# Set-up of a Fourier mixing and gated feed-forward kernel: zeroed rows for halved tables, one product for channel 128, gathers ahead of weights

## The chip, the cores and the metric

The kernel runs on one core of a Trainium2 chip. A core has a matrix engine (TensorE, in the profile PE, with its weight loads as PEld), a vector engine (VectorE, DVE), a scalar engine (ScalarE, ACT), a general engine (GpSimd, POOL), a queue engine that only issues DMAs (SyncE, SP), and 16 DMA engines that all queues share. The metric is the time of one execution on the device in microseconds; lower is better. Each engine works through its own list in order, and semaphores tie the lists together.

## The reference

```python
# x: (8, 3008, 256) float32; w_gate, w_val: (256, 1536); w_out: (1536, 256)
X = np.fft.fft(x, axis=1)                 # along the sequence, 3008
X = np.fft.fft(X, axis=2)                 # along the channels, 256
x = X.real.astype(np.float32).reshape(8 * 3008, 256)
gate = np.maximum(x @ w_gate, 0.0)
val = x @ w_val
return (gate * val @ w_out).astype(np.float32)
```

## The kernel before, in words

**The algebra.** The real part of the two transforms is cosine times cosine minus sine times sine. Because cosine is even and sine odd, row s and row 3008 - s are first added or subtracted ("folded"), then the two halves of the sequence, then channel d and channel 256 - d. What is left is a product of folded rows (F for cosine, G for sine; bf16) with tables tabC and tabS. Its results are U and V, 128 channels by output frequencies. The transform along the channels is a small matrix (TA for cosine, TB for sine) that is multiplied into the weights once: WA = TA^T w and WB = TB^T w for gate and value. Then a tile of the feed-forward part is WA·U + WB·V, and the mirrored frequencies are WA·U - WB·V, made by adding a product with -2V (the tile VM, named CB in the profile) or with WM = -2WB on top of the first sum. Channel 128 has no partner; it is carried in row 0 of V, since row 0 of G is zero.

**Where things lie.** Rows of a half batch are spread over 128 partitions in three thirds t = 0, 1, 2, each with two rows a (or "par") in a partition: XD[p, r, t, a, d] holds row 1 + 2(128t + p) + a of half r, and XG holds the mirrored rows, with a reversed. AA is XG + XD. The last third has 120 partitions of rows and one more, 120, for row 0. Two rows are their own mirrors, row 752 (partition 119, a = 1) and row 0 (partition 120, a = 1). In the kernel before both XD and XG hold them, so they are counted twice, and ScalarE multiplies those two rows of the tables of column c = 5 (t = 2, par = 1) by a half: wv is 1 below partition 119 and 0.5 from there (lines 323 to 324 for the odd frequencies, 460 to 462 for the even ones, wv itself in lines 343 and 344).

**The set-up, in order of the lists.** The schedule is written out by hand; nothing reorders it. SP and ACT issue the upward rows and the plain rows of the first third, then SP the plain rows of the second third, row 0 twice (load_row_0), its mirror and a filling of the unused partitions 121 to 127. POOL makes index vectors and issues gathers of the mirrored rows (load_mirror, L117): two for the second third, then a memset of one element of XD (hold, L113), on which SP's load of the last third waits, then the first gate weights (load_w, L297), the two gathers of the last third, the first value weights, and later the rest of the weights and wo. The first third isn't gathered: TensorE turns it around by a product with a reversed unit matrix (turn, L351). VectorE computes quotients for the angles, md for TA and TB, and for each third AA (L405 or L415, and L406 or L416 for the two end channels), F for both halves (channels, L395 and L393) and G (channels_g, L399). TensorE makes the angles of the odd frequencies (angle, L315 and L316), ScalarE their sines and cosines (L319 to L321).

**The first transform** (dft_first, lines 556 to 614) makes U and V of batch 0 for the odd frequencies. It runs the thirds in order. In each third the list has products for U (k = 0, F with tabC), for V (k = 1, G with tabS) and the channel-128 products (nyquist, L570: one column of F as weights, output row 0 of V's bank), the latter for each half r. Because a channel-128 product may come first, V's banks are opened by two products with zeros (L592). combine (L586) makes the first third of WA and WB from the raw weights; both calls stand ahead of the last third's part. Then ScalarE copies one sum (es), VectorE adds and subtracts (L546) into U and V, and ScalarE makes VM for segment 0 from V (minus_v, L473). The first tiles (first_tile, L887 and L889) follow at once; the mirrored product of a tile (mirror, L804) needs VM.

**Behind it, on POOL.** Once VectorE is through with the thirds (it sets go, L420), POOL folds the even frequencies of batch 0 (lines 434 to 444) and then runs turns_and_rows: the rows of batch 1, the products kvec·us for the even tables (even_turns, L431 and L432), VM of segment 1 and the gathers of batch 1. The even tables are made between the first tiles, by VectorE (L456, L458) and ScalarE (L457, L459, and L461 for the halving). For later batches fold_steps issues load_rows and load_row_0 for the batch after.

Of the kernel before, what the change touches and what calls it, by code (L numbers as in the profile page):

```python
# [34 lines left out]
def kernel(  # L35
# [55 lines left out]
    def load_rows(b, ts=range(3)):  # L91
        for t in ts:
            n = (128, 128, 120)[t]
# [3 lines left out]
    def load_row_0(b):  # L97
        for r in range(2):
            nc.sync.dma_start(out=XD[120:121, r, 2], in_=dram(x, (b * S + r * H) * D, [[0, 1], [0, 2], [1, D]]))
# [4 lines left out]
    def load_spare():  # L104
        for X in (XD, XG):
            nc.sync.dma_start(out=X[121:128, :, 2, :, :].rearrange("p r a d -> p r (a d)"),
                              in_=dram(x, 512 * D, [[2 * D, 7], [H * D, 2], [1, 2 * D]]))
# [68 lines left out]
    def fold_steps(b):  # L176
# [15 lines left out]
        for t in range(3):  # L192
            for i in range(2):
                steps.append((1.1, lambda i=i, t=t: fold_pq(e, p, i, t)))
                if (t, i) == (1, 0) and b + 1 < B:
                    steps.append((0.0, lambda: (load_rows(b + 1), load_row_0(b + 1))))
# [22 lines left out]
    load_row_0(0)  # L219
# [14 lines left out]
    wv = single("wv", [128, 1])  # L234
# [59 lines left out]
    load_rows(0, (2,))  # L294
# [3 lines left out]
    load_w(0, 0)  # L298
    for r in range(2):
        load_mirror(0, 2, r)  # L300
    load_w(1, 0)
# [10 lines left out]
    def angle(n, c):  # L312
# [9 lines left out]
        if c == 5:  # L322
            for tab in (tabC, tabS):
                steps.append(lambda tab=tab: act(tab[r, 5, odd_k], tab[r, 5, odd_k], ACTF.Copy, scale=wv[r]))
# [12 lines left out]
    quotient(4)  # L337
    nc.vector.tensor_scalar(ums[:], pidx[:], scalar1=1.0 / D, op0=ALU.mult, scalar2=None)
# [4 lines left out]
    nc.vector.tensor_scalar(wv[:], pidx[:], scalar1=119.0, op0=ALU.is_lt, scalar2=0.5, op1=ALU.mult)  # L343
    nc.vector.tensor_scalar(wv[:], wv[:], scalar1=0.5, op0=ALU.add, scalar2=None)
# [51 lines left out]

    def channels_g(p, r, t):
# [3 lines left out]
    for t in range(3):  # L401
        n = ROWS[1][t]
        p = slice(0, n)
        if t:
# [3 lines left out]
            for r in range(2):  # L408
                channels(p, r, t)
            for r in range(2):  # L410
                channels_g(p, r, t)
        else:
            nc.vector.memset(GG[1][:].rearrange("p i t q d -> p (i t q) d")[:, :, 0:1], 0.0)
            for r in range(2):
# [3 lines left out]
                channels(p, r, t)  # L418
                channels_g(p, r, t)
# [14 lines left out]
    nc.gpsimd.tensor_copy(go[:, 1:2], go[:, 0:1])  # L434
    hold(slice(0, 3))
    nc.gpsimd.memset(GG[0][:].rearrange("p i t q d -> p (i t q) d")[:, :, 0:1], 0.0)
    for t in range(3):
        p = slice(0, ROWS[1][t])
        for i in range(2):
            nc.gpsimd.tensor_tensor(XG[p, i, t], AA[p, 0, t, :, D:0:-1], AA[p, 1, t, :, 0:D], op=SIGN[i])  # L440
# [676 lines left out]
```

## Time and profile before

| what | value |
|---|---|
| median of 3 runs | 636.41 us (636.18 to 636.57) |
| the profiled execution: its time, its span | 636.55 us, 634.8 us |
| instructions | 12470 |
| DMA | 66.38 MB, mean 105 GB/s |
| first product of the first DFT (L564) starts | 10.00 us |
| first product of the tiles (L887) starts | 19.99 us |
| first mirrored product, with VM (L804), starts | 21.87 us |
| wo asked for, landed | 15.46 us, 15.2 us later |

The span runs from the first to the last instruction in the record of one execution; the rest of that execution's time lies around it. Times of instructions below are counted from the start of the span. In a timeline a line gives start, length, engine, line of the kernel, operation, output and input, and in brackets how long the engine had been idle and what ended that; "issue" there means that nothing which the record shows ended it. Matmuls overlap, so their spacing, not their length, is what each costs.

### The profile page before, as it was taken

The numbers are of one execution on the slowest core, as the hardware profiler recorded it, in microseconds if no ns is written. First come the engines' busy times: TensorE is split into PE (matmuls) and PEld (weight loads), VectorE is DVE, ScalarE is ACT, GpSimd is POOL, SyncE is SP. The second block draws the span as 40 slices with busy tenths as digits, with TensorE's granted clock in tenths as the row PEclk, the third lists the DMA queues.
The fourth block names the chain that finished last, engine by engine and source line by source line (L and its number), as shares of the span: only waits on it lengthen the run. The fifth ranks groups of instructions, "written<-read, shape, count | busy, mean of one in ns | idle before, by whom it ended". The sixth has DMA issues, their size and how long they took to land.

```text
span 634.8 us, 12470 instructions
## 1 busy us (share of the span) xinstructions
PE 622.9 (98%) x4098; PEld 400.3 (63%) x4145; DVE 553.0 (87%) x981; ACT 449.1 (71%) x813; POOL 507.1 (80%) x494
## 2 busy tenths in 40 slices
PE   8999999999999999999999999999999999999997
PEld 3466666566666666666666666666666666666666
DVE  7896576998999999988999999898899989999991
ACT  7787667777777777777677777776777777777752
POOL 8986992898999998898889989699886566666660
PEclk9999999999999999999999999999999999999999
DMA  9953754615272426314272425311221111211122
GB/s 238 209 178 102 188 172 126 183 67 148 82 193 93 128 76 166 128 48 141 72 201 78 140 76 114 74 60 39 72 60 37 42 59 55 59 40 46 52 58 84
DMA packets 64017, 66.38 MB, mean 105 GB/s; under 512 B 19705, under 2 KB 46905, under 8 KB 63952
## 3 DMA queue, kind: packets, MB, share of 16 engines
q1 hardware_dynamic: 59536, 60.02, 33.1%
q0 software_dynamic: 3984, 4.92, 3.9%
q8 instruction: 32, 0.52, 0.4%
q10 hardware_dynamic: 432, 0.66, 0.3%
q14 instruction: 33, 0.27, 0.1%
HBM read 41.83 MB, written 34.13 MB: 120 GB/s over the span
## 4 chain that ended last, share of the span: by engine, by line
PE 91%; DVE 5%; issue 2%; ACT 1%; DVEq 0%; ACTq 0%
PE o L712 36%; PE v L799 10%; PE v L804 10%; PE g L938 8%; PE p L945 8%; PE v L798 7%; PE d L529 4%; DVE h L834 3%; PE p L804 1%; PE p L798 1%; PE p L799 1%; DVE r L949 1%; PE v L351 1%; DVE h L823 1%; PE d L640 0%
## 5 line engine op out<-in xcount | busy, mean ns | idle before, releaser
L950 POOL TENSOR_TENSOR r<-r 128x512 f32<-128x512 f32 (+1 forms) x252 | 314.3, 1252 | 99.8 <-DVE r L949 99.4
L834 DVE SCALAR_TENSOR_TENSOR h<-r,v 128x512 bf16<-128x512 f32 (+1 forms) x504 | 318.6, 674 | 40.0 <-PE v L804 27.9
L712 PE MATMUL o<-wo,h 128*128 128x256 bf16 x2172 | 330.9, 272 | 0.3 <-issue 0.3
L712 PEld LDWEIGHTS <-h 128*128 128x128 bf16 x2220 | 216.8, 98 | 113.7 <-issue 2.3
L933 ACT ACTIVATE p<-CB,b 128x512 f32<-128x512 bf16 (+1 forms) x252 | 172.5, 684 | 73.3 <-DVE r L949 71.7
L941 ACT COPY r<-g 128x512 f32<-128x512 f32 (+1 forms) x252 | 145.4, 577 | 66.9 <-PE g L938 58.7
L949 DVE SCALAR_TENSOR_TENSOR r<-r,p 128x512 f32<-128x512 f32 (+1 forms) x252 | 169.0, 670 | 0.6 <-ACT r L941 0.6
L799 PE MATMUL v<-V,WB 128*128 128x512 bf16 (+3 forms) x296 | 108.6, 367 | 2.3
L804 PE MATMUL v<-V,WM 128*128 128x512 bf16 (+1 forms) x252 | 94.4, 375 | 2.0 <-DVE h L834 1.6
L938 PE MATMUL g<-V,WM 128*128 128x512 bf16 (+1 forms) x252 | 94.5, 375 | 0.4 <-ACT r L941 0.3
L945 PE MATMUL p<-U,WA 128*128 128x512 bf16 (+1 forms) x252 | 94.5, 375 | 0.0
L798 PE MATMUL v<-U,WA 128*128 128x512 bf16 (+3 forms) x252 | 91.9, 365 | 0.0
L823 DVE TENSOR_TENSOR h<-r,v 128x376 bf16<-128x376 f32 (+1 forms) x88 | 45.1, 543 | 19.6 <-PE v L804 12.0
L798 PEld LDWEIGHTS <-WA 128*128 128x128 bf16 x347 | 33.8, 97 | 41.0 <-issue 12.3
L725 ACT COPY os<-o 128x512 f32<-128x512 f32 x92 | 52.5, 572 | 5.0 <-issue 4.5
L799 PEld LDWEIGHTS <-WB 128*128 128x128 bf16 x347 | 33.8, 97 | 34.1 <-DVE WB L385 0.6
L150 POOL TENSOR_TENSOR XG<-XG,XD 128x510 f32<-128x510 f32 x42 | 52.8, 1265 | 0.0
L814 ACT ACTIVATE r<-p 128x376 f32<-128x376 f32 (+1 forms) x80 | 38.2, 486 | 18.3 <-PE p L804 8.8
L158 POOL TENSOR_TENSOR AA<-XG 128x510 f32<-128x510 f32 x42 | 45.3, 1089 | 0.0
L938 PEld LDWEIGHTS <-WM 128*128 128x128 bf16 x252 | 24.6, 98 | 6.4 <-issue 1.0
L945 PEld LDWEIGHTS <-WA 128*128 128x128 bf16 x252 | 24.6, 98 | 3.4 <-issue 0.5
L804 PEld LDWEIGHTS <-WM 128*128 128x128 bf16 x252 | 24.6, 98 | 2.8
(182 smaller groups left out, 424.4 us busy)
## 6 DMA issues: line engine op xcount, KB each, us to landing
out_dram<-os SPq DMA_DIRECT2D x124, 128.0 KB
xr<-in_x_dram SPq DMA_DIRECT2D x12, 768.0 KB
XG<-xr SPq DMA_DIRECT2D x12, 768.0 KB
XD<-in_x_dram SPq DMA_DIRECT2D x15, 512.0 KB
out_dram<-os SPq DMA_DIRECT2D x35, 112.0 KB
XD<-in_x_dram SPq DMA_DIRECT2D x8, 480.0 KB
CB<-ch SPq DMA_DIRECT2D x7, 376.2 KB
out_dram<-os SPq DMA_DIRECT2D x13, 96.0 KB
```

What stands on the lines that cost most here:

```text
L150: e.tensor_tensor(XG[p, r, t, ::-1, 1:D], XG[p, r, t, ::-1, 1:D], XD[p, r, t, :, D - 1:0:-1], op=ALU.add)
L712: nc.tensor.matmul(st["p"][0:m, q, :], lhsT=lhs(f), rhs=wo[:, f, :], start=(f == 0 and not (early and q)), stop=(f == NF - 1), skip_group_ ...
L798: nc.tensor.matmul(bank[:, 0:st["n"]], lhsT=WA[i][:, st["f"]], rhs=st["us"], start=True, stop=False)
L799: nc.tensor.matmul(bank[:, 0:st["n"]], lhsT=WB[i][:, st["f"]], rhs=st["vs"], start=False, stop=True)
L804: nc.tensor.matmul(bank[:, 0:st["n"]], lhsT=W[i][:, st["f"]], rhs=v, start=False, stop=True, skip_group_check=True)
L834: nc.vector.scalar_tensor_tensor(half_h(st, sign), in0=st["s"][1 + sign][:, 0:n], scalar=0.0, in1=st["v"][:, 0:n], op0=ALU.max, op1=ALU.mult)
L933: nc.scalar.activation(st["p"][:, 0:st["n"]], st["c"], ACTF.Copy, scale=b2[:, st["fi"]:st["fi"] + 1])
L938: nc.tensor.matmul(st["g"][:, 0:n], lhsT=WM[0][:, st["f"]], rhs=st["vs"], start=True, stop=True)
L941: nc.scalar.copy(q[:, 0:n], st["g"][:, 0:n])
L945: nc.tensor.matmul(st["p"][:, 0:n], lhsT=WA[0][:, st["f"]], rhs=st["us"], start=False, stop=True, skip_group_check=True)
L949: nc.vector.scalar_tensor_tensor(sp[:, 0:n], in0=q[:, 0:n], scalar=-0.5, in1=st["p"][:, 0:n], op0=ALU.mult, op1=ALU.add)
L950: nc.gpsimd.tensor_tensor(sm[:, 0:n], sp[:, 0:n], q[:, 0:n], op=ALU.add)
```

## The change

- The halving of table rows goes: wv, its two instructions, and the four ScalarE operations that multiply tabC and tabS of c = 5. Instead XD is zero wherever XG already holds a self-mirrored row: VectorE zeroes XD[96:128, :, 2, 1, :] once, and the plain rows of the last third are loaded as 112 partitions of whole pairs (load_rows), then 8 partitions for a = 0 and 7 for a = 1 (load_last), so that partitions 119 and 120 of a = 1 stay zero in all batches. load_row_0 goes, load_last takes its place for every batch. For batch 0 the loads of the last third move behind the memset in the listing, in front of ums; the hold on POOL stays where it was.
- Channel 128 of both halves goes into one product: VectorE subtracts the two halves' channel 128 (half_128 into hy), ScalarE doubles the difference into bf16 (whole_128 into ny), and nyquist runs once for each third and par instead of once for each half too. The two products with zeros go; V's own first product opens its bank.
- The gathers of the last third are asked for ahead of the first gate weights on POOL.
- In dft_first the order is written anew: products loop over r outside and par inside; nyquist comes after U's products in the second and third thirds; combine(0) stays ahead of the last third, combine(1) goes into it in two parts; U is finished before V's last products are issued; WB of the gate is copied by VectorE, and WA of the value by ScalarE (before it was the other way around).
- VM of segment 0 is made by POOL, inside the fold of the even frequencies (fold_even, now called after dft_first), between its first and second operation, instead of by ScalarE.

```diff
     def load_rows(b, ts=range(3)):
-            n = (128, 128, 120)[t]
+            n = (128, 128, 112)[t]
...
-    def load_row_0(b):
-        for r in range(2):
-            nc.sync.dma_start(out=XD[120:121, r, 2], in_=dram(x, (b * S + r * H) * D, [[0, 1], [0, 2], [1, D]]))
+    def load_last(b):
+        for a in range(2):
+            n = (8, 7)[a]
+            nc.sync.dma_start(out=XD[112:112 + n, :, 2, a, :], in_=dram(x, (b * S + 1 + 2 * (256 + 112) + a) * D, [[2 * D, n], [H * D, 2], [1, D]]))
...
-                    steps.append((0.0, lambda: (load_rows(b + 1), load_row_0(b + 1))))
+                    steps.append((0.0, lambda: (load_rows(b + 1), load_last(b + 1))))
...
     hold(slice(2, 3))
-    load_rows(0, (2,))
...
-    load_w(0, 0)
     for r in range(2):
         load_mirror(0, 2, r)
+    load_w(0, 0)
     load_w(1, 0)
...
-        if c == 5:
-            for tab in (tabC, tabS):
-                steps.append(lambda tab=tab: act(tab[r, 5, odd_k], tab[r, 5, odd_k], ACTF.Copy, scale=wv[r]))
...
     quotient(5)
     quotient(4)
+    nc.vector.memset(XD[96:128, :, 2, 1, :], 0.0)
+    load_rows(0, (2,))
+    load_last(0)
...
-    nc.vector.tensor_scalar(wv[:], pidx[:], scalar1=119.0, op0=ALU.is_lt, scalar2=0.5, op1=ALU.mult)
-    nc.vector.tensor_scalar(wv[:], wv[:], scalar1=0.5, op0=ALU.add, scalar2=None)
...
+    def half_128(p, t):
+        nc.vector.tensor_tensor(hy[p, t], AA[p, 0, t, :, 128], AA[p, 1, t, :, 128], op=ALU.subtract)
+
+    def whole_128(t):
+        p = slice(0, ROWS[1][t])
+        nc.scalar.mul(ny[p, t], hy[p, t], 2.0)
...
             for r in range(2):
                 channels(p, r, t)
+            half_128(p, t)
...
+    def fold_even():
...
             for i in range(2):
+                if (t, i) == (0, 1):
+                    minus_v(nc.gpsimd, 0)
...
-        if c == 5:
-            steps += [lambda tab=tab: act(tab[r, 5, even_k], tab[r, 5, even_k], ACTF.Copy, scale=wv[r])
-                      for tab in (tabS, tabC)]
...
-        for par in (1, 0):
-            nc.tensor.matmul(bank[1, par][:, 0:NJ], lhsT=warm[:, 0:128], rhs=warm[:, 0:NJ], start=True, stop=False, skip_group_check=True)
-        part(0, (0,))
+        products(0, 0, (0,))
+        products(0, 1, (0,))
+        whole_128(0)
         angle(4, 5)
-        part(0, (1,))
+        products(0, 0, (1,))
+        products(0, 1, (1,))
+        nyquist(0)
         angle(5, 4)
-        part(1)
-        combine(0)
-        combine(1)
-        part(2)
+        whole_128(1)
+        products(1, 0, (0, 1))
+        nyquist(1)
+        products(1, 1, (0, 1))
+        combine(0, (0, 1))
+        whole_128(2)
         nc.scalar.copy(*whole(WA[0], raw[0]))
-        nc.vector.tensor_scalar(*whole(WA[1], raw[2]), scalar1=1.0, op0=ALU.mult, scalar2=None)
+        products(2, 0, (0, 1))
+        combine(1, (0,))
+        ends[0][1](1)
+        ends[0][1](0)
+        evict.pop(0)()
         nc.vector.tensor_scalar(m2[:], pidx[:], scalar1=1.0, op0=ALU.min, scalar2=-2.0, op1=ALU.mult)
...
+        sums[0]()
+        by_vector(WB[0], raw[1])
+        nc.scalar.copy(*whole(WA[1], raw[2]))
+        nyquist(2)
+        products(2, 1, (0, 1))
+        combine(1, (1,))
...
-        minus_v(nc.scalar, 0)
...
     dft_first(U, V)
+    fold_even()
     turns_and_rows()
```

## The prediction

> **What bounds the kernel now.** I read the engines' totals on the page first, then the chain that ended last, cut to the first 60 us because the whole diff lies there, then the timelines of VectorE and of GpSimd (POOL) in the set-up, and last the DMA queues microsecond by microsecond.
>
> ```profile
> PE 622.9 (98%) x4098; PEld 400.3 (63%) x4145; DVE 553.0 (87%) x981; ACT 449.1 (71%) x813; POOL 507.1 (80%) x494
> ```
>
> TensorE is busy for 98% of the span, so a microsecond by which its main stream starts earlier is a microsecond of the total, unless something else holds it later. The chain, from 16 us (start, length, what):
>
> ```profile
> 16.11 0.86 PE v L586 x4
> ...
> 17.24 0.59 PE d L586 x2
> 17.84 0.64 PE p L564 x4
> ...
> 20.26 0.56 DVE V L546
> 20.84 0.61 ACT CB L473
> 21.45 0.38 ACT r L814
> 21.87 0.32 PE p L804
> ...
> 43.70 0.48 ACT r L814
> 44.19 0.50 ACT tabS L461
> ...
> 46.86 0.32 PE p L804
> ```
>
> Two places are not TensorE alone: the hand-over from the first DFT to the tiles (VectorE makes V, ScalarE makes -2V into CB, then the first relu, then the mirrored product), and a ScalarE stretch at 43.7 to 46.9, in which TensorE sits idle for 0.28 and 0.39 us. Just ahead of 17.84 TensorE's weight load waits 0.2 us for VectorE's F of the last third: two chains arrive there almost together. VectorE's own side:
>
> ```profile
> 13.18 0.74 DVE L399 TENSOR_TENSOR G<-AA 128x254 bf16<-128x254 f32 x2
> 15.38 1.22 DVE L405 TENSOR_TENSOR AA<-XG,XD 121x1020 f32<-121x1020 f32 x1 [1.46 <-issue]
> 17.26 0.42 DVE L393 SCALAR_TENSOR_TENSOR F<-AA 121x258 bf16<-121x258 f32 x1
> ```
>
> It is done with the second third at 13.92 and waits 1.46 us, for nothing that an engine does: for data. POOL's timeline says which:
>
> ```profile
> 6.63 0.80 POOL L297 DMA_DIRECT2D h<-in_moe_w_gate_dram  x1
> 7.73 1.21 POOL L117 DMA_INDIRECT XG<-in_x_dram,gidx  x1 [0.30 <-issue]
> 9.24 0.98 POOL L117 DMA_INDIRECT XG<-in_x_dram,gidx  x1 [0.31 <-issue]
> 10.23 0.79 POOL L297 DMA_DIRECT2D h<-in_moe_w_val_dram  x1
> ```
>
> The last third's gathers are asked for behind the first gate weights, in one software queue. The two queues between 9 and 10 us (packets, MB, share):
>
> ```profile
> q1 hardware_dynamic: 112, 0.23, 97.9%
> q0 software_dynamic: 13, 0.01, 6.5%
> ```
>
> The last third's plain rows occupy 9 to 11.2 us; from 11.2 the software queue runs full, first in packets of about 1 KB (weights), from 12.5 to 14 in larger ones (gathers). VectorE starts 1.2 us after these end.
>
> **The change part by part.** All against the profiled execution: 636.55 us, span 634.8, so 1.75 around it; the median of the three runs is 636.41, 0.14 less.
>
> *Gathers first.* The weight issue in front of them took 0.80 us, so they are asked for at about 6.9 and 8.4 and the gate weights at 9.4; the second weight issue (10.23) and all behind it on POOL stay. What is surely gained is 0.8 us; with the weights' transfer (256 KB at the queue's 0.20 MB/us: 1.3 us) behind them too, the data could be there at 13.3. Landing is then 13.3 to 14.6; I take 14.0, the middle.
>
> *VectorE.* The added memset of 32x512 f32: the nearest row is 95x384 in 0.38, so 0.5 (bounds 0.21, the memset of 95x188, and 0.69, the longest 512-wide row nearby); the two wv operations removed give back 0.25. Both lie ahead of the 0.21 us for which L415 waits at 6.66 and the 0.65 us at 8.99, and are gone by then. It delays the absolute value for TA by 0.3 us on ScalarE, which has 0.83 us free at 8.8. Three half_128, 0.16 each by the 128x4 row of L416 (0.43 beside POOL work at most): two come before the last third, 13.92 + 0.3 = 14.2. So L405 starts at 14.25 instead of 15.38, and with the same spacing the last F stands at 16.55 instead of 17.68: 1.13 us.
>
> *SP.* The memset's wait queues load_rows of the last third and both load_last behind VectorE's 5.5; the hold on POOL releases at 6.68 as before (6.71 in the trace), so that wait costs nothing. The two load_last (16 and 14 rows of 1 KB, issue 0.56 to 0.79 by the row-0 loads that they replace) end by 8.3 and queue behind the plain rows, whose data end at 11.2; 3 us to spare before 14.25. For later batches it is five issues either way.
>
> *TensorE up to the last third.* Gone are two products with zeros (0.31 each, at half speed) and, in the first two thirds, four of eight channel-128 products (0.25 of spacing each); combine(1), 0.86, goes behind. Added: nyquist(1) waits for ScalarE's ny, a 0.2 us operation (row 128x1; 0.29 for 128x129) behind angle(5,4). Counting on from 9.38 at the trace's spacings: angle(4,5) done by 10.8, angle(5,4) by 12.3, then F of the second third (13.1, 13.45). ScalarE without the two halvings (0.52 and 0.50) ends the last table at 14.1, ny at 14.25; queued behind that wait are nyquist(1), products(1,1) and combine(0): 14.3 + 0.5 + 0.65 + 0.86 = 16.3. So TensorE is ready as F arrives (16.2 and 16.55).
>
> *The tail.* products(2,0) end at 16.95, combine (0.43) 17.4, two channel-128 products 17.8, products(2,1) 18.5, V's copy on ScalarE 18.9, V on VectorE 19.55 (the WB copy now ahead of it takes 0.65 that fits), the product that uses V at 19.6 instead of 20.86. ScalarE then has no -2V to make: the first relu runs at 20.0 to 20.45. POOL makes -2V in 0.57 (its row for segment 1), 19.6 to 20.2, in time. The mirrored product starts at 20.5 instead of 21.87: 1.37 us.
>
> *What POOL's wait delays.* POOL now stands from 18.9 to 19.6 for V with the rest of fold_even behind it: even_turns' first result comes at 31.65 instead of 31.29, and VectorE wants it (33.22 before) at 31.85. Cover: 0.2 us; without it every tenth goes to the products. wo lands at 30.66 and its first product would be at 31.1: 0.4 us of cover.
>
> *The weights' new place.* No row shows a weight transfer behind four gathers. Three weight rows land 6.0, 6.6 and 6.8 us after their issue: 15.4 to 16.2. TensorE wants them at 15.45, so the cost is 0 to 0.75; the queue holds the same bytes as it did when g4 landed at 15.38, so I take 15.6 and 0.15.
> On that the Trainium skill differs (DMA: Bandwidth & Descriptors, Anatomy of one DMA): about 2.0 us fixed plus bytes by 436 GB/s, an estimate of 2.6 us for 256 KB, which would land at 12.0 and cost nothing; the trace has 6.8 us for this transfer, and I keep to it.
>
> *Even tables.* Of the two removed ScalarE operations (L461) the first, 0.50, is in the chain. Behind it two copies of output (0.96) remain. Between 0 and the 0.67 us that TensorE idles there; I take 0.4.
>
> Sum: 1.37 - 0.15 + 0.4 = 1.6 us. 636.55 - 1.6 = 634.95 beside the profile, 634.8 beside the median. Bounds: 0.6 to 1.4 at the start and 0 to 0.67 at the tables, 0.6 to 2.1 together.
>
> **The rivals.**
>
> *The weights arrive last.* combine(0) now stands ahead of products(2,0), so a landing at 16.2 pushes everything by 0.75: 1.37 - 0.75 + 0.4 = 1.0, 635.4. For: 6.8 us is this very transfer's row, and 3.4 us passed between its issue and its first packets. Against: in those the plain rows had the engines.
>
> *POOL or the tables take it back.* VectorE waits 0.3 to 0.5 for even_turns, or the copies at 45.5 hold TensorE all the same: about 1.1 saved, 635.3. Against: POOL's wait is shorter than what VectorE's late start cost it before (1.12 at 18.44).
>
> *TensorE was the bound up to 17.8 and its savings are eaten by the wait for ny.* Only the tables remain: 636.0. Against: VectorE's 0.2 us at 17.7.
>
> *Slower: the clock drops.* The products of 376 columns start 0.31 us apart until about 10.0 and 0.16 from there, with granted clock 1.00 throughout; so there is a second, slower speed, and it lasted 8.8 us after the first product. The new order leaves TensorE idle at 12.3 to 13.1 and 13.75 to 14.3, where before it ran without a gap. If that sends it back to half speed for as long, 4.4 us are lost: 636.41 - 1.6 + 4.4 = 639.2. It decides (0.2%) from 2.9 us lost, that is 5.8 us at half speed. Against: 0.28 and 0.39 us idle at 45 to 47, and 0.46 at 4.1, were followed by no slower spacing than before.
> The Trainium skill (TensorE: Matmul & The Clock Gate, Part 1) has the rule: half clock after at least one idle window of about 3.4 us. By it gaps of 0.8 us change nothing; no gap so long is in this trace.
>
> **How the numbers follow.** 0.60 for the forecast, 0.15 for late weights, 0.06 for POOL or tables, 0.04 for TensorE as the bound, 0.15 for the clock and anything like it. About 0.2% (1.3 us) is what a measurement here can tell from no change; below 635.1 is faster, so faster 0.60, same 0.25, slower 0.15. The forecast's own range is 634.3 to 635.1, from the upper bound of the sum to the limit of what counts as faster. The whole range starts 0.3 lower, for the spread of the runs (636.18 to 636.57), and reaches to 637.7, where the slower case begins: 634.0 to 637.7 leaves that case's 0.15 out and a few hundredths below.
>
> **What would show it.** L405's second instance starting at 14.0 to 14.6 with under 0.5 us idle ahead of it; the first product with V near 19.6 and the mirrored one near 20.5; no TensorE idle of 0.3 us or more at 42 to 46. Against me: a wait of TensorE for weights at combine(0), VectorE waiting for AA from POOL near 32, or 0.31 us spacing after 12 us.

## The result and the profile after

The changed kernel takes 634.94 us (median of 10 runs, 634.55 to 635.49) where the kernel before takes 636.57 on the same chip (10 runs, 636.18 to 636.7). The ratio is 0.9975, with a 95% interval from 0.9965 to 0.9985. The profiled execution took 634.97 us with a span of 633.2, against 636.55 and 634.8 before: 1.6 us less in both, as forecast. The parts of that sum did not all come out as forecast, and some of them were not in it at all.

The totals of the engines, first part of the changed kernel's page:

```profile
PE 620.3 (98%) x4090; PEld 399.1 (63%) x4137; DVE 553.8 (87%) x983; ACT 446.8 (71%) x811; POOL 507.0 (80%) x495
```

TensorE has eight products fewer and is busy for 2.6 us less. Its share stays at 98%, so the span still follows the start of its main stream.

The chain that ended last, cut to 8 to 48 us (start, length, what):

```profile
8.19 4.82 DMA XG<-in_x_dram,gidx
13.00 0.67 DVE G L405 x2
13.67 0.37 issue
14.04 1.23 DVE AA L411
...
15.57 0.44 DVE F L391
16.01 0.05 issue
16.06 0.83 PE p L575 x4
...
20.42 0.27 PE p L822
...
43.18 0.48 ACT r L832
43.66 0.18 ACT os L742
...
44.63 0.40 ACT r L832
45.03 0.04 issue
45.07 0.32 PE p L822
```

Up to 16 us the chain is data, then VectorE: the last gather, AA, F, and only then TensorE's products of the last third. Before, TensorE's own list (the combines) reached up to 17.84. At the tables there is no sine left in the chain, and of the two idle stretches of TensorE the first (0.28) is gone; the second stands in the timeline of TensorE:

```profile
45.07 0.32 PE L822 MATMUL p<-CB,WB 128*128 128x376 bf16 x1 [0.39 <-ACT r L832]
```

VectorE's timeline around the last third, and POOL's with the gathers:

```profile
12.93 0.74 DVE L405 TENSOR_TENSOR G<-AA 128x254 bf16<-128x254 f32 x2
14.04 1.22 DVE L411 TENSOR_TENSOR AA<-XG,XD 121x1020 f32<-121x1020 f32 x1 [0.37 <-issue]
15.92 0.42 DVE L389 SCALAR_TENSOR_TENSOR F<-AA 121x258 bf16<-121x258 f32 x1
```

```profile
6.89 0.99 POOL L118 DMA_INDIRECT XG<-in_x_dram,gidx  x1 [0.21 <-issue]
8.19 1.01 POOL L118 DMA_INDIRECT XG<-in_x_dram,gidx  x1 [0.30 <-issue]
9.21 0.83 POOL L295 DMA_DIRECT2D h<-in_moe_w_gate_dram  x1
10.01 0.81 POOL L295 DMA_DIRECT2D h<-in_moe_w_val_dram  x1
```

VectorE still waits for data, now 0.37 us instead of 1.46. By the events of its semaphore the last gather landed at 13.96 (15.30 before) and the first gate weights at 14.66 (13.38 before). The queues between 9 and 10 us:

```profile
q1 hardware_dynamic: 134, 0.27, 104.2%
```

Before, this queue moved 0.23 MB in the same microsecond. TensorE's timeline:

```profile
12.65 0.83 PE L575 MATMUL p<-tabC,F 128*128 128x376 bf16 x4 [0.85 <-DVE F L391]
13.75 0.48 PE L581 MATMUL o<-tabC,ny 128*1 128x376 bf16 x2 [0.26 <-ACT ny L401]
14.81 0.59 PE L589 MATMUL v<-h,TA 128*128 128x512 bf16 x2
16.06 0.83 PE L575 MATMUL p<-tabC,F 121*128 121x376 bf16 x4 [0.22 <-DVE F L391]
19.47 0.32 PE L907 MATMUL p<-V,WB 128*128 128x376 bf16 x1
20.36 0.33 PE L822 MATMUL p<-CB,WB 128*128 128x376 bf16 x1
```

The reader sees the two waits of the new order (0.85 and 0.26), combine(0) at 14.81 with no wait for weights, and the mirrored product at 20.36 instead of 21.87. POOL's first result for the even tables, and VectorE's use of it, without a wait:

```profile
31.02 0.51 POOL L441 TENSOR_SCALAR AA<-AA 128x377 f32<-128x377 f32 x1
```

```profile
31.73 0.87 DVE L468 SCALAR_TENSOR_TENSOR AA<-kvec,u,AA 128x377 f32<-128x377 f32 x1
```

Further on I followed VectorE's h products (relu of the gate times the value; there are 600): the k-th of the changed kernel starts earlier than the k-th of before by 1.47 us where before stands at 37 us, by 1.89 at 55, 1.90 at 134, 1.69 at 196 and 473, and 1.46 at 610. So 1.9 us were gained by 55 us and 0.44 of them given back in two steps, at 170 and 566 us, far from anything that the change touches. Behind 610 us, 0.37 came back at one place, and the last h product is 1.83 us earlier, as is the end of TensorE's last product (629.36 instead of 631.19). In this execution 0.26 of that was lost again until the last output had landed.

### The profile page after: what moved, and what is told of

Its sections match the earlier page's. It is cut to its first block, busy times and chain, and to the rows that moved or that the text cites. A ratio compares the mean times of both kernels' runs of the same rounds, so it can differ in the third digit from the quotient of the medians.

```text
span 633.2 us, 12459 instructions
## 1 busy us (share of the span) xinstructions
PE 620.3 (98%) x4090; PEld 399.1 (63%) x4137; DVE 553.8 (87%) x983; ACT 446.8 (71%) x811; POOL 507.0 (80%) x495
## 4 chain that ended last, share of the span: by engine, by line
PE 88%; DVE 5%; DMA 2%; issue 2%; ACT 1%; POOL 1%; SPq 0%; DVEq 0%; ACTq 0%; POOLq 0%
PE o L729 35%; PE v L817 10%; PE v L822 10%; PE g L956 8%; PE p L963 8%; PE v L816 7%; PE d L538 4%; DVE h L852 3%; DMA xr<-in_x_dram 2%; PE p L822 1%; PE p L816 1%; PE p L817 1%; DVE r L967 1%; DMA XG<-in_x_dram,gidx 1%; DVE h L841 1%
```

## The experiments

The runs are before or the changed kernel with one thing altered; the last two add instructions whose output nothing reads. "Mirrored" is the start of the first mirrored product, and "at 55" and "at 610" are how far the h product stands behind (+) or ahead (-) of the same one of before, where that is at 55 and at 610 us. "Clock" is the time at which a trace's record of TensorE's granted clock begins, with 1.0. The record has nothing before that, which a view of a stretch prints as 1.00 (so the prediction's "granted clock 1.00 throughout"); but until then the products of 376 columns start 0.31 us apart, and from then on 0.16. All columns but the first two are of one profiled execution each.

| run | median us (range) | ratio to before, 95% | clock | AA of last third | mirrored | at 55 | at 610 |
|---|---|---|---|---|---|---|---|
| before (profile) | | | 10.57 | 15.38 | 21.87 | 0 | 0 |
| the change | 634.94 (634.55 to 635.49) | 0.9965 to 0.9985 | 8.02 | 14.04 | 20.36 | -1.89 | -1.46 |
| e1_gathers | 636.46 (636.02 to 636.84) | 0.9992 to 1.0010 | 9.63 | 14.29 | 21.53 | -0.34 | -0.34 |
| e2_no_gathers | 635.34 (634.99 to 635.77) | 0.9975 to 0.9993 | 7.73 | 14.36 | 20.68 | -1.58 | -1.18 |
| e3_zero_rows | 636.16 (635.89 to 636.98) | 0.9990 to 1.0008 | 7.66 | 14.87 | 21.27 | -1.06 | -0.17 |
| e4_scalar_vm | 634.61 (634.41 to 634.72) | 0.9959 to 0.9982 | 9.05 | 14.05 | 20.49 | -1.85 | -1.45 |
| e5_order | 636.55 (636.08 to 637.81) | 0.9998 to 1.0017 | 9.26 | 15.53 | 22.00 | +0.15 | +0.33 |
| e6_two_products | 635.54 (635.15 to 636.01) | 0.9975 to 0.9994 | 10.09 | 14.01 | 20.76 | -1.50 | -0.60 |
| e7_w00_last | 635.25 (635.21 to 635.65) | 0.9976 to 0.9994 | 9.69 | 13.87 | 20.93 | -1.32 | -0.93 |
| e8_iota_late | 634.76 (634.41 to 634.87) | 0.9963 to 0.9983 | 8.12 | 14.18 | 20.50 | -1.75 | -1.34 |
| e9_split_only | 636.01 (635.79 to 636.63) | 0.9989 to 1.0007 | 7.08 | 14.99 | 21.39 | -0.42 | -0.56 |
| e10_105_rows | 634.46 (634.23 to 634.98) | 0.9963 to 0.9982 | 8.88 | 14.07 | 20.38 | -1.88 | -1.57 |
| e11_four_more | 634.26 (634.12 to 634.41) | 0.9951 to 0.9978 | 8.94 | 13.92 | 20.23 | -2.03 | -1.94 |
| e12_products_seven | 634.59 (634.38 to 634.85) | 0.9958 to 0.9982 | 9.89 | 13.84 | 20.58 | -1.67 | -1.60 |

The kernel before, run beside them, had medians of 636.34 to 636.43, where it has 636.57 beside the change. The change itself was not run beside the others: e4, e8 and e10, whose traces follow the same course as its own, have medians 0.2 to 0.5 us below its 634.94. A few tenths between the change's median and that of another run can therefore not be put down to an edit by themselves; where each is taken against before beside it, this is said.

### One part alone

**e1_gathers**: before, with the gathers of the last third ahead of the first gate weights and nothing else.

```diff
-    load_w(0, 0)
     for r in range(2):
         load_mirror(0, 2, r)
+    load_w(0, 0)
     load_w(1, 0)
```

> The kernel before, with only the last third's gathers put ahead of the first gate weights. Theory (two chains meet: VectorE waiting for the gathers, and TensorE's list with both combines ahead of the last third's products): the data land near 14.0, VectorE starts the last third's AA at 14.0 instead of 15.38, but TensorE reaches the last third's products at 17.5 to 17.8 as before, so the first mirrored product stays within 0.3 us of 21.87 and the total is 0 to 0.3 us less than before. If TensorE's clock switches up earlier in an execution, its list is shorter there and up to 0.7 us more is gained in that one. Rival (VectorE's wait was the bound and the parts add up): 1.1 us less on their own, the mirrored product near 20.8.

The last gather landed at 14.21, and the total did not move (636.46). VectorE's and TensorE's timelines of this run:

```profile
14.29 1.22 DVE L405 TENSOR_TENSOR AA<-XG,XD 121x1020 f32<-121x1020 f32 x1 [0.24 <-issue]
```

```profile
9.88 0.48 PE L564 MATMUL p<-tabC,F 128*128 128x376 bf16 x2
...
17.33 0.81 PE L564 MATMUL p<-tabC,F 121*128 121x376 bf16 x4
```

AA is 1.1 us earlier, but the products that need it are only 0.34 us earlier, and they start without a wait: TensorE comes out of its own list (the combines) at 17.33. That its list ends earlier than before's is not the gathers' doing either. The clock came to full speed at 9.63 us instead of 10.57, as the first two products of U show: here they take 0.48 us together, and in before

```profile
10.00 0.76 PE L564 MATMUL p<-tabC,F 128*128 128x376 bf16 x2
```

So in the old order the data's gain has nowhere to go, unless the clock happens to shorten TensorE's list.

**e3_zero_rows**: before, with the zero rows alone (load_rows of 112, load_last, the memset; wv and the four halvings gone).

```diff
-            n = (128, 128, 120)[t]
+            n = (128, 128, 112)[t]
...
+    nc.vector.memset(XD[96:128, :, 2, 1, :], 0.0)
+    load_rows(0, (2,))
+    load_last(0)
...
-        if c == 5:
-            for tab in (tabC, tabS):
-                steps.append(lambda tab=tab: act(tab[r, 5, odd_k], tab[r, 5, odd_k], ACTF.Copy, scale=wv[r]))
```

> The kernel before, with only the zero rows in place of the halved tables. Theory: the two ScalarE operations of the set-up were hidden, so the first mirrored product stays at 21.7 to 21.9; at the even tables the 0.28 us idle of TensorE goes and 0.3 to 0.5 us are gained; total 0.3 to 0.5 us less than before. Rival (the tables' operations were hidden there too, or the load in three pieces costs as much): no difference, under 0.1 us.

The total is 0.2 us lower than before's, inside the interval of no change, and the mirrored product is not where it was expected. AA starts 0.51 us earlier, although the gathers are asked for as before (the last one landed at 14.79 instead of 15.30), the mirrored product 0.60 earlier, and 1.06 us were gained by 55 us. The 0.46 that come at the even tables, between 45 and 49 us, are the zero rows': every run with zero rows gains 0.40 to 0.47 there, and no other does. The 0.60 at the start are not theirs alone. The full clock came 2.9 us earlier than in before's profile; with before's clock TensorE's list, which is the same, would have reached the last third at about the 17.67 of before (an estimate from before's trace), and not at 16.89. Of the 1.06, 0.89 were lost again by 610 us, in three steps at 67, 422 and 468 us. What these are is the subject of the last two runs. Read from the total alone, this run would have said that the zero rows are worth nothing.

**e5_order**: before, with the single channel-128 product, the new order of dft_first and VM by POOL, but without zero rows and with the weights ahead of the gathers.

```diff
+    def half_128(p, t):
+        nc.vector.tensor_tensor(hy[p, t], AA[p, 0, t, :, 128], AA[p, 1, t, :, 128], op=ALU.subtract)
...
-        combine(0)
-        combine(1)
-        part(2)
+        combine(0, (0, 1))
+        whole_128(2)
...
+        products(2, 0, (0, 1))
+        combine(1, (0,))
```

> The kernel before, with the one product for channel 128, the new order of the first transform and VM of segment 0 on POOL, but neither the zero rows nor the earlier gathers. Theory: AA of the last third starts at 15.3; TensorE is ready for it early and waits; behind it the tail is shorter because ScalarE has no VM to make: the first mirrored product at 21.4 to 21.6, total 0.3 to 0.5 us less than before. Rival (TensorE's list was the bound): the mirrored product at 20.8 or earlier, 1 us less without the gathers.

No change in the median (636.55), where 0.3 to 0.5 us less had been expected. TensorE's timeline shows two waits:

```profile
15.19 0.48 PE L588 MATMUL o<-tabC,ny 128*1 128x376 bf16 x2 [1.22 <-ACT ny L405]
...
17.55 0.67 PE L582 MATMUL p<-tabC,F 121*128 121x376 bf16 x3 [0.27 <-DVE F L395]
```

ScalarE still makes the halvings ahead of ny, so TensorE waits 1.22 us there (0.26 in the changed kernel), and the last third's data are as late as ever (AA at 15.53). A shorter list of TensorE alone brings nothing either.

One thing in this run bears on the rival of the clock. Six of its eleven executions took 636.08 to 636.55 us, with a mean granted clock of 0.999 or 1.0; the other five took 637.0 to 637.81, with 0.997. No other execution of the study has less than 0.998. The only other value in any trace's record is 0.5, and 0.997 over 635 us would be 3.2 to 4.4 us at 0.5 (an estimate from these figures). This kernel is also the one whose TensorE waits longest in the set-up, 0.95 us up to 13.13 and 1.22 up to 15.19. That the waits cost it the clock is not shown, since none of these five executions left a trace.

So the mirrored product moves by -0.34, -0.60 and +0.13 us with one part each, together -0.81, and by -1.51 with all of them; and the first two of these were had beside an earlier clock. The remaining 0.7 us or more exist only when the data, ScalarE and TensorE's list are all early. The kernel's time agrees: +0.1, -0.2 and +0.2 alone (against before's medians beside them), -1.6 together.

### One part taken back

**e2_no_gathers**: the changed kernel with the first gate weights ahead of the gathers again (the diff of e1_gathers, backwards).

> The changed kernel with only the gathers put back behind the first gate weights. Theory: AA of the last third starts at 15.3 again, the first mirrored product at 21.4 to 21.6; of the whole gain 0.3 to 0.5 us is left at the start and 0.3 at the even tables, total 0.6 to 0.8 us less than before (0.8 to 1.0 more than the changed kernel). Rival (the new order and the clock did it, the gathers nothing): within 0.3 us of the changed kernel.

The last gather landed at 14.28 and AA started at 14.36, when the gathers had been asked for as late as before the change. I had expected 15.3: the landing had become earlier by itself. Between these two profiles the gathers' order is worth 0.3 us of landing (14.28 to 13.96) and 0.3 at the mirrored product. Single profiles scatter, though: e3_zero_rows, with the same loads in the same order as e2, has 14.79, and seven profiles with 112 rows and the gathers first have 13.57 to 14.10. Of the total it is worth 0.4 us (635.34 to 634.94), or 0.6 with each against before beside it (1.0 and 1.6 less); the larger part of the gain stays without it.

**e8_iota_late**: the changed kernel with the index vector of the last third behind the gathers on POOL, so that they are asked for another 0.6 us earlier.

```diff
-    for t in (1, 2):
-        iota(urow[0:1, 2 * t:2 * t + 2], [[1, 2], [2, 128]], 256 * t + 1, 0)
-    nc.gpsimd.memset(urow[0:1, 5, 120:121], 0.0)
+    iota(urow[0:1, 2:4], [[1, 2], [2, 128]], 257, 0)
     load_mirror(0, 1, 1)
...
     for r in range(2):
         load_mirror(0, 2, r)
+    iota(urow[0:1, 4:6], [[1, 2], [2, 128]], 513, 0)
+    nc.gpsimd.memset(urow[0:1, 5, 120:121], 0.0)
     load_w(0, 0)
```

> The changed kernel with POOL's index row of the last third (0.5 us) and its small memset made behind the gathers instead of between them, so that the second, third and fourth gather are asked for 0.55 us earlier. Theory: the last gather lands near 13.4, VectorE's wait of 0.37 us goes, and the start gains 0.3 us: 0.3 us less than the changed kernel. Rival (the plain rows that occupy the queues until 11.2 set the landing): no difference in landing or total.

POOL's timeline:

```profile
6.29 1.02 POOL L118 DMA_INDIRECT XG<-in_x_dram,gidx  x1 [0.21 <-issue]
7.61 0.97 POOL L118 DMA_INDIRECT XG<-in_x_dram,gidx  x1 [0.30 <-issue]
```

They are asked for 0.6 us earlier and land at 14.10 instead of 13.96: nothing gained. So here it is no longer the time of asking that sets the landing. That the other loads on the DMA engines set it, as the rival had it, is the likely reading; this run does not show it.

**e7_w00_last**: the changed kernel with the first gate weights also behind the first value weights.

```diff
     for r in range(2):
         load_mirror(0, 2, r)
-    load_w(0, 0)
     load_w(1, 0)
+    load_w(0, 0)
```

> The changed kernel with the first gate weights asked for behind the first value weights, so that they land at about 15.95 instead of 14.66. This is the price of the rival of late weights. Theory: combine(0) stands ahead of the last third's products, TensorE waits for the weights until 15.9 and 0.86 us of combine(0) lie behind that, so the last third's first product moves from 16.06 to 16.8: 0.6 to 0.8 us more than the changed kernel. Rival (the weights have a cover of more than 1.2 us): no difference.

TensorE's timeline:

```profile
15.79 0.59 PE L589 MATMUL v<-h,TA 128*128 128x512 bf16 x2 [0.56 <-DMA h<-in_moe_w_gate_dram]
```

The weights landed at 15.65, which is the value that the prediction had taken for the change itself, TensorE waited 0.56 us, the mirrored product came 0.57 later and the total is 0.3 higher (0.5 with each against before beside it, and 0.5 by the h product at 610 us). The prediction had put a landing at 15.6 at 0.15 us: it had TensorE ask for the weights at 15.45, and it asks at 14.81 in the changed kernel and 15.23 here. So late weights cost more than forecast; in the changed kernel they are not late, by 0.15 us (landed at 14.66).

**e4_scalar_vm**: the changed kernel with VM of segment 0 by ScalarE again.

```diff
-                if (t, i) == (0, 1):
-                    minus_v(nc.gpsimd, 0)
...
         nc.scalar.copy(*whole(WB[1], raw[3]))
+        minus_v(nc.scalar, 0)
```

> The changed kernel with VM of segment 0 made by ScalarE again, after its last weight copy, and not by POOL. Theory: ScalarE is free at 19.55, makes VM until 20.1, and the first relu moves from 19.82 to 20.1: the first mirrored product at 20.6 instead of 20.36, total 0.2 to 0.3 us more than the changed kernel. Rival (POOL's wait for V costs what ScalarE saves, through the even tables): the same as the changed kernel or 0.2 us less.

634.61, not slower than the change, where 0.2 to 0.3 us more had been expected. ScalarE's timeline shows why:

```profile
19.46 0.61 ACT L480 ACTIVATE CB<-V,m 128x376 bf16<-128x376 bf16 x1
19.97 0.47 ACT L831 ACTIVATE r<-p 128x376 f32<-128x376 f32 x1
```

The relu starts at 19.97, and the mirrored product at 20.49: 0.13 us later than with POOL, and this is gone by 55 us (-1.85 against -1.89). Handing VM to POOL is worth nothing that these runs can tell.

**e6_two_products**: the changed kernel with twelve channel-128 products again, without half_128 and whole_128.

```diff
-                nc.tensor.matmul(bank[1, par][0:1, 0:NJ], lhsT=ny[rows, t, par:par + 1], rhs=tabC[rows, 2 * t + par, odd_k],
-                                 start=False, stop=False, skip_group_check=True)
+                for r in range(2):
+                    nc.tensor.matmul(bank[1, par][0:1, 0:NJ], lhsT=FF[1][rows, r, t, par, 128:129], rhs=tabC[rows, 2 * t + par, odd_k],
+                                     start=False, stop=False, skip_group_check=True)
```

> The changed kernel with channel 128 of each half in a product of its own again (twelve instead of six, no difference and no doubling), in the new order. Theory: in the first two thirds TensorE has idle time to cover them and the wait for the doubled value goes; in the last third two more of 0.2 us each stand ahead of V's products: 0.3 to 0.5 us more than the changed kernel, the first mirrored product at 20.7 to 20.9. Rival (all six cost their spacing): 1.2 to 1.5 us more; or none, because ScalarE's copies of the weights bound the tail: the same.

635.54, 0.6 us above the change (0.8 with each against before beside it); but the mirrored product is only 0.40 later, and by 610 us the distance to the changed kernel is 0.86. This run too loses on the way: 0.9 us at 67, 422 and 468 us, the same three places as e3_zero_rows.

### Why the gathers land earlier by themselves

The part of the zero rows that stands in the way of the gathers is the load of the last third's plain rows: 120 partitions before, 112 and then 8 and 7 in the change. The 120 landed at 12.41 and the 112 at 11.48. Two other things changed on SP's queue: row 0's loads are gone, and load_spare, which the list of the change does not name, fills eight partitions of XD for a = 0 only, where it filled seven for both a.

**e9_split_only**: before, with this one load cut at 112.

```diff
-            n = (128, 128, 120)[t]
+            n = (128, 128, 120 if b else 112)[t]
...
+            if t == 2 and not b:
+                nc.sync.dma_start(out=XD[112:120, :, 2].rearrange("p r a d -> p r (a d)"),
+                                  in_=dram(x, (1 + 2 * (256 + 112)) * D, [[2 * D, 8], [H * D, 2], [1, 2 * D]]))
```

> Before, with only the set-up's load of the last third's plain rows cut in two: 112 partitions in one DMA and 8 in a second behind it on SP's queue. Theory A (the shape of this load sets when the gathers land; the zero rows brought the earlier landing only through it): the 112 rows land near 11.5 us instead of 12.4, the last gather near 14.7 instead of 15.30, the last third's AA starts near 14.8 instead of 15.38. The total stays within 0.3 us of before, 636.1 to 636.6 on the same chip, since TensorE's list is as long as before. Theory B (the landing came earlier because row 0's loads and the second spare load are gone from SP's queue): the last gather lands at 15.2 to 15.4 and AA starts at 15.3 to 15.5. The total is before's within 0.2 under B.

**e10_105_rows**: the changed kernel with the cut at 105 instead of 112.

```diff
-            n = (128, 128, 112)[t]
+            n = (128, 128, 112 if b else 105)[t]
...
+        m = 112 if b else 105
         for a in range(2):
-            n = (8, 7)[a]
+            n = 120 - m - a
```

> The changed kernel, with the set-up's load of the last third's plain rows cut at 105 partitions instead of 112, the other 15 and 14 rows in the two small loads: the same bytes in as many DMAs. Theory A (the shape sets the landing): the 105 rows land 0.5 to 0.9 us later than the 11.48 of the 112, the last gather 0.3 to 0.7 later than 13.96, and the total is 635.0 to 635.5 where the changed kernel has 634.7 to 634.9. Theory B (the shape is nothing, the landing came earlier by what left SP's queue): last gather within 0.2 of 13.96, total within 0.2 of the changed kernel.

In e9_split_only the 112 rows landed at 11.66, the last gather at 14.91 and AA started at 14.99, between the two theories and nearer to A's; the total fell by 0.3, not to be told from nothing. The queues between 9 and 10 us have 0.29 MB where before had 0.23:

```profile
q1 hardware_dynamic: 140, 0.29, 106.0%
```

In e10_105_rows the 105 rows landed at 11.45 and the last gather at 13.98, as in the changed kernel: theory A, as I had put it there, fails. The total of 634.46 lies below what either theory had named. I had thought of how many DMA engines carry the load. Of before's 120 rows one semaphore event came at 7.22, half a microsecond after the issue, and so did one of the 105 rows (7.34), but none of the 112 (first at 10.72). The Trainium skill (DMA: Bandwidth & Descriptors, Why a DMA increments its semaphore by 16 and not by 1) reads that as follows: a transfer goes to the largest number of engines up to 16 that divides its rows, and the issuing engine counts those without a share at once. By that 15, 15 and 16 engines carried data, and the events agree. But then a share is 8, 7 and 7 rows of an engine, and the three landings (12.41, 11.45, 11.48) follow that, not the count of engines. This reading was formed after the run, and was not tried by a further one. What the traces show is an order without overlap. The load itself landed 5.6 to 6.1 us after its issue in three profiles with 120 rows, and 4.2 to 5.5 us in ten with 112. With the gathers behind the weights, the last of them landed at 15.30 and 15.45 with 120 rows in one load (before, e5_order) and at 14.91, 14.79 and 14.28 with 112 (e9, e3, e2); with the gathers first, at 14.21 with 120 (e1) and at 13.57 to 14.10 with 112 (seven profiles). Of these pairs only before and e9 differ in the cut alone; its 0.4 us rest on one profile each, and profiles with the same loads differ by up to 0.5.

### Where 0.4 to 0.9 us went later

The changed kernel loses time in two steps of 0.21 and 0.23 us, e3_zero_rows and e6_two_products in steps of 0.2 to 0.35 at other places than it does, but at the same ones as each other. I numbered the entries that the record has for VectorE, waits included, from 0. e3 and e6 have three fewer ahead of such a place than the changed kernel and e2, e4, e7, e8 and e10; these six lose at the same instructions, whatever else differs. Over all fourteen profiled executions, from place 100 on, VectorE's work behind a wait that ended last started 0.05 us after the wait (median of about 2,700). It started more than 0.2 us after it in 22 cases, by 0.39 to 0.41, and all 22 stand at place 63, 191, 319 and so on, every 128; at these places no such wait was shorter. On ScalarE the same places show 0.32 to 0.33 us in 37 of 37, where the median is 0.04.

**e11_four_more**: the changed kernel with four small memsets more on VectorE, in an idle microsecond at 56 us.

```diff
+    late = single("late", [128, 8])
+    more.setdefault((1, 9), []).extend(lambda i=i: nc.vector.memset(late[:, i:i + 1], 0.0) for i in range(4))
```

> The changed kernel with four memsets of 128x1 more on VectorE, of a tile that nobody reads, behind the h product at 56 us, where VectorE is idle for 1.0 us; they take about 0.06 us each. Theory A (a wait of VectorE costs 0.35 us more where the instruction behind it stands at place 63, 191, 319 and so on, every 128, of VectorE's stream): four places on, none of these places falls behind a wait any more; in the changed kernel two do, at 170 and 566 us. Both stalls of 0.40 us are gone, nothing new comes, and the total is 634.3 to 634.7, 0.2 to 0.5 under the changed kernel's. Theory B (the stalls at 170 and 566 us belong to that work, such as a collision with GpSimd at that moment): they stay where they are, and the total is the changed kernel's plus 0 to 0.25: 634.8 to 635.2.

**e12_products_seven**: e6_two_products with seven of them at the same place, which gives the later instructions the same places as in e11.

```diff
+    more.setdefault((1, 9), []).extend(lambda i=i: nc.vector.memset(late[:, i:i + 1], 0.0) for i in range(7))
```

> The changed kernel with its twelve channel-128 products of before (run alone, that took 635.54), and seven memsets of 128x1 more at the same place, so that VectorE's instructions behind it stand at the same places as in the run with four more. Theory A: the three stalls of that kernel, at 67, 422 and 468 us, are gone, and with them 0.5 to 0.9 us: 634.6 to 635.0. What is left against the run with four more, 0.2 to 0.5 us, is the price of the twelve products themselves. Theory B: 635.4 to 635.8, with the stalls where they were.

VectorE's timeline of the changed kernel, at the two places where it loses:

```profile
168.68 0.65 DVE L967 SCALAR_TENSOR_TENSOR r<-r,p 128x481 f32<-128x481 f32 x1
169.78 1.23 DVE L852 SCALAR_TENSOR_TENSOR h<-r,v 128x481 bf16<-128x481 f32 x2 [0.45 <-PE v L817]
...
565.69 1.29 DVE L852 SCALAR_TENSOR_TENSOR h<-r,v 128x512 bf16<-128x512 f32 x2 [0.42 <-PE v L817]
```

and of e11_four_more (its lines are numbered two higher):

```profile
56.31 0.08 DVE L776 MEMSET late<- 128x1 f32 x4
...
168.72 0.65 DVE L969 SCALAR_TENSOR_TENSOR r<-r,p 128x481 f32<-128x481 f32 x1
169.48 1.23 DVE L854 SCALAR_TENSOR_TENSOR h<-r,v 128x481 bf16<-128x481 f32 x2
...
565.08 1.28 DVE L854 SCALAR_TENSOR_TENSOR h<-r,v 128x512 bf16<-128x512 f32 x2
```

The idle 0.45 and 0.42 us are gone, with no line of the work changed. For e6_two_products and e12_products_seven, the place at 422 us:

```profile
422.34 1.28 DVE L847 SCALAR_TENSOR_TENSOR h<-r,v 128x512 bf16<-128x512 f32 x2 [0.91 <-PE v L812]
```

```profile
421.58 1.28 DVE L849 SCALAR_TENSOR_TENSOR h<-r,v 128x512 bf16<-128x512 f32 x2 [0.55 <-PE v L819]
```

The 0.55 that is left there is in before as well; 0.36 went. The added instructions took away the stalls that they were aimed at, in both kernels. The totals are 634.26 against 634.94, and 634.59 against 635.54, in each case with no run of the one as slow as the fastest of the other. For e12 that stands against before beside each too (1.84 us less, and 0.86 for e6). For e11 it is not the total that shows it, but the trace: e10_105_rows, which has both stalls, took 634.23 to 634.98 on another chip, e11 634.12 to 634.41. By the h product between 55 and 610 us, e11 lost 0.09 us where the change lost 0.43. Both totals lie at the lower end of theory A's ranges, 0.04 and 0.01 us below them, and outside theory B's. One clause of it failed: at 63 us e11 lost 0.2 us for good, behind a wait that had ended during the product before it, which my count of places had not taken in. e11_four_more has the lowest median of this study.

It also corrects two readings. The twelve products cost 0.33 us (634.59 against 634.26), as much as the mirrored product was late, and not the 0.6 that e6_two_products showed. And the zero rows are worth more than the 0.2 us that their total showed: 0.4 to 0.5 at the even tables for certain, and up to the 1.06 that e3_zero_rows had at 55 us, of which the early clock may have a part. That is worked out from traces; a padded version of e3 was not run.

What makes these places is argued, not shown. The page of the changed kernel has two queues that bring instructions:

```profile
q8 instruction: 32, 0.52, 0.4%
...
q14 instruction: 33, 0.27, 0.1%
```

They moved 0.79 MB for 12459 instructions, 63 bytes each. A packet of q14 is 8.2 KB, so 129 instructions, which is close to the distance of the places. The Trainium skill (Runtime: NRT & Kernel Launch, Instruction fetch mechanics) says that an engine's instructions are refilled in blocks of 256 and that crossing a boundary is mostly hidden. If the places are such boundaries, the measurement differs: every 128 on VectorE and ScalarE, and 0.35 and 0.28 us more behind a wait. No run here tried the cause.

## Why the prediction came out right, step by step

- **Gathers first.** Taken: asked for at 6.9 and 8.4, landing at 14.0. Measured: 6.89 and 8.19, 13.96. The number was right for half the reason. In before the step alone does bring 1.1 us (14.21 in e1), but in the changed kernel e2 has 14.28 without it: the 0.8 us that were "surely gained" were 0.3 there, since the load of the plain rows had brought the gathers forward too.
- **SP.** The wait cost nothing, as put down (the load is issued at 6.71 in both). What failed is that the new loads were costed as so many issues with time to spare, and put at no effect on anything else. I counted their issues and not when the load of the plain rows ends: cut at 112 it landed 0.9 us earlier, and the gathers behind it 0.4 (e9).
- **VectorE.** Memset 0.48 (0.5 taken), half_128 0.15 (0.16). It was ready at 13.67, not 14.2, since the second third's AA began at 10.26 instead of 10.60, where I had counted 0.3 us of delay. AA began at 14.04 (14.25), and the last F ended at 16.34 (16.55).
- **TensorE up to the last third.** It was to be ready as F arrives, at 16.2 to 16.55. It was ready at 15.84 and waited 0.22 for F. Both waits of the new order came, each about half a microsecond earlier than put (12.3 to 13.1 and 13.75 to 14.3 forecast; idle for 0.85 up to 12.65 and 0.26 up to 13.75). TensorE had come to full speed at 8.02, where I had counted on from before's trace (10.57), and VectorE was ahead too.
- **The tail.** Product with V at 19.47 (19.6), mirrored product at 20.36 (20.5): 1.51 us in place of 1.37. The new maker of VM had been taken as a part of that gain; e4 shows that it isn't.
- **POOL.** It waited 0.88 us for V, even_turns' first result came at 31.53 (31.65), and VectorE's use of it at 31.73 had no wait. The cover of 0.2 us was just what was left.
- **Weights.** They landed at 14.66, 5.45 us after their issue, against 15.6 taken, and cost nothing (0.15 taken). The Trainium skill's fixed time plus bytes (DMA: Bandwidth & Descriptors, Anatomy of one DMA) gave an estimate of 2.6 us for this transfer: right in that there was no cost, but not in the time. The bounds of 15.4 to 16.2 came from rows with the longer plain load ahead, and left out the 5.8 us of the first value weights (10.23 to 16.05 in before). Two errors met here: the weights came 0.9 us earlier than taken, and TensorE asked for them at 14.81, 0.6 us earlier than the 15.45 taken. That it cost nothing was luck, with 0.15 us to spare; e7 shows that 15.65 costs 0.57 us at the mirrored product.
- **Even tables.** 0.4 taken out of 0 to 0.67; 0.42 measured (the lead grows from 1.47 at 37 us to 1.89 at 55).
- **What was missing.** 0.44 us lost at 170 and 566 us, 0.37 won at 617, where before has such a stall (place 1599 of its entries) and the changed kernel has none, and 0.26 lost at the very end. 1.51 + 0.42 - 0.44 + 0.37 - 0.26 is 1.60. The forecast of 1.6 was hit because a set-up that went 0.3 us better than forecast paid for losses that were not in it. That part of the agreement is luck; that the start and the even tables carry the gain is not.

Of the rivals, late weights and POOL are refuted by the lines above. TensorE as the bound with a wait for ny is what e5 shows (1.22 us), but only as long as the halvings stand ahead of ny. In the changed kernel's profile the clock did not drop: after idle times of 0.85 and 0.26 us the products of 376 columns still start 0.16 us apart, in line with the rule of the Trainium skill (TensorE: Matmul & The Clock Gate, Part 1) that was weighed there. The five executions of e5 with a granted clock of 0.997 leave it open whether longer waits can cost it.

## What to carry to other kernels

Where two chains arrive at one place together, changes of one part each measure as nothing, and it takes the trace, not the total, to see that each shortened its own chain. Before two single profiles of a set-up are compared, see where the clock came to full speed in each: here it lay anywhere between 7.1 and 10.6 us. Before a few tenths of a microsecond in a total are put down to an edit, follow one repeated instruction through both traces: a step in the distance far from the edit is another cause, and a handful of idle instructions more or less can decide it. When a load stands ahead of what the kernel waits for, look at when it lands and how its rows are cut, not only at its bytes and its issue; that it is the rows of one DMA engine that count is a reading that was not tried.

## What was not expected of the hardware

- Work directly behind a wait on VectorE starts 0.39 to 0.41 us after it, and not 0.05, at every 128th place of its instructions; 0.32 to 0.33 and not 0.04 on ScalarE.
- A load of 120 rows landed 5.6 to 6.1 us after its issue (three profiles), one of 112 rows 4.2 to 5.5 (ten), and one of 105 rows 4.8 (one).
- TensorE's step from products 0.31 us apart to 0.16 comes at 7.08 to 10.57 us, depending on the execution; the changed kernel's profile has it at 8.02 and before's at 10.57. The medians are over many executions, the traces are not. Before's own gain from an earlier step is small in this case, since VectorE's F of the last third arrives at the same time as TensorE's list ends (17.67).
